# Keeping one and a half V tiles instead of one between two decoder layers, with reordered visits and smaller helper operations

## The chip, the cores and the metric

The kernel runs on one core of one Trainium2 chip. The metric is the device time of one execution, in microseconds (us). Executions of most of the kernels here agree within about 0.1%, so medians of four or more runs are compared. Each round of experiments ran on one chip beside runs of the kernel before; kernels of different rounds ran on different chips, and are compared because the kernel before agreed there (medians 2558.78 to 2559.24 us).

## The reference

Two blocks, A (attention over a cache) and B (a feed-forward network), run alternately, twice, on 8 rows of 640 numbers. Both attention blocks read the same caches: 8 batches x 32 heads x 4096 keys x 128, bf16, for K and for V, 536.9 MB.

```python
def _A_ref(x, k_cache, v_cache, wq, wo):
    q = (x @ wq).reshape(B, Sq, Hq, Dh).transpose(0, 2, 1, 3)     # Sq = 1, 32 heads of 128
    scores = jnp.einsum("bhqd,bhkd->bhqk", q, k) * (Dh ** -0.5)
    o = jnp.einsum("bhqk,bhkd->bhqd", _softmax(scores), v)
    return o.transpose(0, 2, 1, 3).reshape(B, Sq, Hq * Dh) @ wo
def _B_ref(x, w1, w2):
    return jnp.maximum(x @ w1, 0) @ w2                              # 640 -> 1728 -> 640
x = A_x
x = x + _A_ref(_layernorm(x), ...);  x = x + _B_ref(_layernorm(x), ...)
x = x + _A_ref(_layernorm(x), ...);  x = x + _B_ref(_layernorm(x), ...)
```

## The kernel before

The work is a list of 256 visits: 2 layers x 8 batches x 16 pairs of heads. A visit needs a K tile and a V tile of 2 MB each (128 partitions x 64 keys x 128). They pass through a ring of four slots of 16 KB per partition. DVE multiplies the K tile by the query in place; PE sums it ("folds" it) with identity matmuls; a softmax over two visits follows; three visits later PE applies the weights to V ("attend"). A batch's layer-1 visits are put among the next batch's layer-0 visits, and the V tile of pair 15 stays on chip from layer 0 to layer 1, so that layer 1 need not load it.

```python
KEEP = 1
...
def load_v(v):
    layer, b, hp = visits[v]
    if hp in keep:
        if layer == 1:
            V_tiles[v] = kept.pop((b, hp))
            return
        V_tiles[v] = kept[b, hp] = rpool.tile([P, J, Dh], BF16, name=f"V_keep{keep.index(hp)}")
    else:
        V_tiles[v] = kv.tile([P, J, Dh], BF16, name="V_sb", tag="kv")
    nc.sync.dma_start(out=V_tiles[v], in_=pair_src(A_v_cache, b, hp))
...
    for i in range(NV + LAG):            # LAG = 3, v = i - LAG   (cut: conditions)
        mult/fold(i, parts 0, 1)
        reduce_s(i - 1); softmax_a(blk); softmax_d(v // 2); scale_o(v - 1); add_y(v - 2)
        mult/fold(i, parts 2, 3)
        load_first(i, v)                 # K tile i + 2, into the slot of K tile i
        softmax_b(blk)
        o_sb = attend(v)
        load_second(i, v)                # V tile v + 2, into the slot of V tile v
        softmax_c(blk); gather_o(v, o_sb); project_o(v - 1)
```

A K slot comes free when its last fold ends; a V slot when its attend ends.

## Time and profile before

| | before |
|---|---|
| time, median of 13 runs in all | 2558.92 us |
| DMA: bytes, share of 16 engines' span | 1071.93 MB, 99.4% |
| rate from 165 to 2500 us | 425 GB/s |
| DVE wait for K tiles | 1013.8 us, 4.0 us per visit |
| last V tile landed, to the end of the span | 2539.40 us, 17.60 us |

First the page of the kernel before. The digits are busy tenths in 40 equal slices, GB/s is what DMA moved in each; then come the data queue (packets, MB, share of 16 engines' span) and the chain of work that ended last, by engine.

```profile
span 2557.0 us, 36318 instructions
PE 1922.1 (75%) x15406; PEld 867.4 (34%) x15406; DVE 1484.9 (58%) x2451; ACT 512.8 (20%) x1604; POOL 2.0 (0%) x15
...
DMA  9999999999999999999999999999999999999996
GB/s 395 415 413 426 427 426 426 426 426 420 426 427 424 424 423 426 426 422 426 423 426 426 426 420 427 425 426 425 419 427 425 426 425 420 427 427 425 425 419 292
...
q1 hardware_dynamic: 81808, 1071.93, 99.4%
...
DMA 61%; PE 22%; DVE 14%; issue 2%; ACT 1%; SPq 0%; DVEq 0%; ACTq 0%
```

DMA is full in every slice but the last; PE and DVE are not. The chain shows 61% for DMA because it steps through load, multiply, fold and next load of the same slot.

The timeline of the end (start us, us, what, and in brackets the idle time before it) shows the serial tail:

```profile
2539.40 1.91 PE L365 MATMUL o_ps<-V_sb,P 128*8 128x512 bf16 x16 [1.66 <-DMA V_sb<-in_A_v_cache_dram]
...
2542.06 1.28 ACT L162 ACT_TABLE_LOAD   x1
...
2545.76 0.26 ACT L162 ACTIVATE lnv<-ch_ps,eps_c 128x1 f32<-128x1 f32 x1 [2.42 <-PE ch_ps L157]
2546.04 1.28 ACT L164 ACT_TABLE_LOAD   x1
2547.33 0.20 ACT L164 ACTIVATE rstd<-lnv 128x1 f32<-128x1 f32 x1
...
2554.66 0.31 SPq L510 DMA_DIRECT2D out_dram<-xo  x1
```

Of the two activation-table loads the first is done while others work; the second stands in the chain.

### The profile page before, as it was taken

To read this page: it belongs to the slowest core of one execution; us is meant where nothing else is said; L and a number is where in the kernel's file an instruction comes from. 1 tells how busy PE (TensorE), PEld (TensorE's weight loads), DVE (VectorE), ACT (ScalarE), POOL (GpSimd) and SP (SyncE) were. 2 spreads that over 40 slices of the span, in tenths; PEclk is the share of its full clock that TensorE was granted. 3 is DMA by queue.
4 is the path that set the end of the run, shared out by engine and by line. 5 is a ranking of instruction groups with operands and counts; after the bars stand their busy time and mean duration, and the time that the engine had idled before them with its cause. 6 is when DMAs were issued, how large, how long until landed. Compare 5 with 4: busy or idle time off the path is not lost.

```text
span 2557.0 us, 36318 instructions
## 1 busy us (share of the span) xinstructions
PE 1922.1 (75%) x15406; PEld 867.4 (34%) x15406; DVE 1484.9 (58%) x2451; ACT 512.8 (20%) x1604; POOL 2.0 (0%) x15
## 2 busy tenths in 40 slices
PE   6657776787777867778777787778777788777776
PEld 2223332343333423334333343333333244323333
DVE  5446565656656556556566565555565565655653
ACT  1112221122112212122111221112221122112212
POOL 0000000000000000000000000000000000000000
PEclk8878888898989888888888888888888888888887
DMA  9999999999999999999999999999999999999996
GB/s 395 415 413 426 427 426 426 426 426 420 426 427 424 424 423 426 426 422 426 423 426 426 426 420 427 425 426 425 419 427 425 426 425 420 427 427 425 425 419 292
DMA packets 81970, 1074.24 MB, mean 420 GB/s; under 512 B 8256, under 2 KB 14096, under 8 KB 17296
## 3 DMA queue, kind: packets, MB, share of 16 engines
q1 hardware_dynamic: 81808, 1071.93, 99.4%
q8 instruction: 120, 1.97, 0.3%
q14 instruction: 42, 0.34, 0.0%
HBM read 1071.88 MB, written 0.01 MB: 419 GB/s over the span
## 4 chain that ended last, share of the span: by engine, by line
DMA 61%; PE 22%; DVE 14%; issue 2%; ACT 1%; SPq 0%; DVEq 0%; ACTq 0%
DMA K_sb<-in_A_k_cache_dram 60%; PE s_ps L303 18%; DVE K_sb L293 12%; DVE S_sb L314 1%; PE o_ps L365 1%; PE q_ps L277 1%; ACT P L341 1%; PE ch_ps L208 1%; DMA V_sb<-in_A_v_cache_dram 0%; ACT o_sb L370 0%; DVE mrow L318 0%; PE ch_ps L188 0%; PE blk_ps L320 0%; PE blk_ps L332 0%; PE y_ps L389 0%
## 5 line engine op out<-in xcount | busy, mean ns | idle before, releaser
L293 DVE TENSOR_TENSOR K_sb<-K_sb,qb 128x2048 bf16<-128x2048 bf16 x1024 | 1205.7, 1220 | 1018.1 <-DMA K_sb<-in_A_k_cache_dram 1013.8
L303 PE MATMUL s_ps<-K_sb,ident_b 128*128 128x512 bf16 x4096 | 1266.7, 458 | 379.8 <-DVE K_sb L293 359.0
L303 PEld LDWEIGHTS <-ident_b 128*128 128x128 bf16 x4096 | 452.7, 113 | 1064.0 <-issue 695.4
L370 ACT CAST o_sb<-o_ps 104x512 bf16<-104x512 f32 x256 | 149.8, 585 | 807.0 <-PE o_ps L365 802.9
L365 PE MATMUL o_ps<-V_sb,P 128*8 128x512 bf16 x3840 | 258.0, 381 | 2.1 <-DMA V_sb<-in_A_v_cache_dram 2.1
L334 ACT ACTIVATE nmax<-blk_ps 128x4 f32<-128x4 f32 x128 | 22.2, 173 | 1067.2 <-PE blk_ps L332 1067.2
L341 ACT ACTIVATE P<-S_sb,nmax 64x64 bf16<-64x64 f32 x512 | 186.8, 365 | 9.1
L314 DVE TENSOR_REDUCE S_sb<-s_ps 128x64 f32<-128x512 f32 x256 | 175.1, 684 | 3.6 <-PE s_ps L303 2.3
L376 PE MATMUL oT_ps<-dsel,o_sb 104*128 104x2 bf16 x1024 | 64.4, 167 | 115.9 <-ACT o_sb L370 115.9
L348 PE MATMUL blk_ps<-lrow,ones_f 128*128 128x4 f32 x256 | 49.9, 265 | 119.3 <-ACT P L341 119.3
L365 PEld LDWEIGHTS <-P 128*8 128x8 bf16 x4096 | 98.7, 86 | 95.2 <-issue 47.6
L376 PEld LDWEIGHTS <-o_sb 104*128 104x128 bf16 x1024 | 44.2, 98 | 183.8 <-ACT o_sb L370 183.6
L389 PE MATMUL y_ps<-oT,wo_sb 128*128 128x1 bf16 x2560 | 99.8, 163 | 0.3 <-DVE oT L381 0.3
L348 PEld LDWEIGHTS blk_ps<-lrow,ones_f 128*128 128x128 f32 x256 | 38.7, 191 | 176.0 <-ACT P L341 173.5
L341 ACT ACTIVATION_READ_ACCUMULATOR P<-S_sb,nmax 64x1 f32 x512 | 94.6, 185 | 0.0
L389 PEld LDWEIGHTS <-wo_sb 128*128 128x128 bf16 x2560 | 82.5, 96 | 0.4 <-DVE oT L381 0.4
L282 ACT CAST qb<-q_ps 128x512 bf16<-128x512 f32 x64 | 37.4, 585 | 141.0 <-PE q_ps L277 141.0
L332 PEld LDWEIGHTS blk_ps<-diag,ones_f 2*128 2x128 f32 x256 | 37.4, 182 | 54.6 <-issue 48.7
L277 PE MATMUL q_ps<-wq_sb,xln 128*64 128x512 bf16 x320 | 53.0, 474 | 2.7 <-DMA wq_sb<-in_A_wq_dram 2.7
L332 PE MATMUL blk_ps<-diag,ones_f 2*128 2x4 f32 x256 | 48.7, 258 | 0.6 <-DVE diag L328 0.6
L277 PE MATMUL q_ps<-wq_sb,xq 128*64 128x512 bf16 x320 | 46.1, 423 | 0.0
L320 PE MATMUL blk_ps<-ident_f,mrow 128*2 128x128 f32 x128 | 45.9, 358 | 0.0
(53 smaller groups left out, 561.7 us busy)
## 6 DMA issues: line engine op xcount, KB each, us to landing
K_sb<-in_A_k_cache_dram SPq DMA_DIRECT2D x256, 2048.0 KB, 12.9
V_sb<-in_A_v_cache_dram SPq DMA_DIRECT2D x240, 2048.0 KB, 16.5
V_keep<-in_A_v_cache_dram SPq DMA_DIRECT2D x8, 2048.0 KB, 17.2
wq_sb<-in_A_wq_dram SPq DMA_DIRECT2D x4, 1280.0 KB, 19.0
wo_sb<-in_A_wo_dram SPq DMA_DIRECT2D x4, 1280.0 KB, 24.7
w_sb<-in_B_w_dram SPq DMA_DIRECT2D x1, 2160.0 KB, 28.0
w_sb<-in_B_w_dram SPq DMA_DIRECT2D x1, 2080.0 KB
w_sb<-in_B_w_dram SPq DMA_DIRECT2D x1, 80.0 KB, 31.1
```

The lines of the kernel that those rows point to most:

```text
L277: nc.tensor.matmul(q_ps[hh * HP : (hh + 1) * HP], lhsT=_free(xl[:, c, col : col + 1], [(0, HP)]), rhs=wv[:, c, g, :, hh, :], start=(c == 0 ...
L293: nc.vector.tensor_tensor(out=kk, in0=kk, in1=_free(qb_tiles[i][:, lo : lo + DW], [(0, J), (1, DW)]), op=ALU.mult)
L303: nc.tensor.matmul(s_tiles[i], lhsT=ident_b, rhs=K_tiles[i][:, :, lo : lo + RW], start=(part == 0 and k == 0), stop=(part == NQT - 1 and k ...
L314: nc.vector.tensor_reduce(out=S_tiles[k][:, j, :], in_=s_tiles.pop(i), axis=AX.X, op=ALU.add)
L320: nc.tensor.transpose(out=blk_ps[k][:2, :P], in_=mrow, identity=ident_f)
L332: nc.tensor.matmul(gmax, lhsT=ones_f[:2, :], rhs=diag.rearrange("n j h -> n (j h)"), start=True, stop=True)
L341: nc.scalar.activation(out=P2[k % 2][r, j, :, hh], in_=S[r, j, :], func=ACT.Exp, bias=nmax[r, j, hh : hh + 1], scale=inv_sqrt_dh, accum_ou ...
L348: nc.tensor.matmul(L_ps, lhsT=ones_f, rhs=lrow2[k % 2].rearrange("p j h -> p (j h)"), start=True, stop=True)
L365: nc.tensor.matmul(o_ps[32 * c : 32 * c + 8, :], lhsT=P2[k % 2][:, j, 4 * g : 4 * g + 4, :], rhs=V[:, 4 * g : 4 * g + 4, :], start=(g < 4) ...
L370: nc.scalar.copy(out=o_sb, in_=o_ps[:104, :])
L376: nc.tensor.matmul(oTp_tiles[v], lhsT=o_sb[:, i, :], rhs=dsel[:104, i, :], start=(i == 0), stop=(i == 3))
L389: nc.tensor.matmul(y_tiles[v][:, c : c + 1], lhsT=wo_sb[:, 2 * hp + hh, c * P : (c + 1) * P], rhs=oT[:, hh : hh + 1], start=(hh == 0), sto ...
```

## The change

The intent: fewer bytes. Besides pair 15's V tile, half of pair 14's stays on chip (32 of 64 keys per partition, 8 KB). To make room, small buffers shrink (identity and ones in bf16 or as one column, fewer double buffers). At the same time the visit is reordered: all multiplies and folds of a visit run back to back, the last 32 columns as two parts of 16, and the small operations follow. Layer norm takes a square root and a reciprocal instead of logarithm and exponential; the softmax maximum goes through PE in bf16; the transposes of input and output become one matmul each.

```diff
-KEEP = 1
+KEEP = ((0, 64), (1, 32))
+PARTS = (32, 32, 32, 16, 16)
@@ load_v
-        if hp in keep:
-            if layer == 1:
-                V_tiles[v] = kept.pop((b, hp))
-                return
-            V_tiles[v] = kept[b, hp] = rpool.tile(...)
-        else:
-            V_tiles[v] = kv.tile(...)
-        nc.sync.dma_start(out=V_tiles[v], in_=pair_src(A_v_cache, b, hp))
+        kk = keep.get(hp, 0)
+        src = pair_src(A_v_cache, b, hp)
+        pieces = []
+        if kk and layer == 0:
+            kept[b, hp] = rpool.tile([P, kk, Dh], BF16, name=f"V_keep{hp}")
+            nc.sync.dma_start(out=kept[b, hp], in_=src[:, :kk, :])
+        if kk:
+            pieces.append((0, kk, kept[b, hp]))
+        if kk < J:
+            V = kv.tile([P, J, Dh], BF16, name="V_sb", tag="kv")
+            nc.sync.dma_start(out=V[:, kk:, :], in_=src[:, kk:, :])
+            pieces.append((0, J, V))
+        V_tiles[v] = pieces
@@ layer norm
-            nc.scalar.activation(out=lnv, in_=st["var"], func=ACT.Ln, bias=eps_c, scale=1.0 / D)
-            nc.scalar.activation(out=r, in_=lnv, func=ACT.Exp, scale=-0.5)
+            nc.scalar.activation(out=st["std"], in_=st["var"], func=ACT.Sqrt, bias=eps_c, scale=1.0 / D)
+            nc.vector.reciprocal(out=rstd, in_=st["std"])
@@ the visit, in order (cut: conditions)
-  mult/fold(parts 0, 1); reduce_s; softmax_a; softmax_d; scale_o; add_y(v - 2); mult/fold(parts 2, 3)
-  load_first; softmax_b; attend; load_second; softmax_c; gather_o; project_o
+  score(i)  (five parts, back to back); take_q; load_first; softmax_c; attend; load_second
+  reduce_s; softmax_a; softmax_d; scale_o; project_o; softmax_b; add_y(v - 1); project_q; gather_o
... (cut: bf16 identity and ones, x as [P, B, DC], one PSUM tile for o and y, single transposes)
```

More of the change, by code (lines that the diff above doesn't have):

```diff
@@ L72 @@
     w2_sb = wres.tile([P, FC, D], BF16, name="w2_sb")
-    x_bf = sm.tile([B, D], BF16, name="x_bf", tag="row", bufs=1)
-    nc.sync.dma_start(out=x_bf, in_=A_x.rearrange("b s d -> (b s) d"))
+    x_bf = sm.tile([B * DC, P], BF16, name="x_bf", tag="row", bufs=1)
+    nc.sync.dma_start(out=x_bf, in_=A_x.rearrange("b s (c p) -> (b s c) p", p=P))
     wq_sb = wres.tile([P, DC, HD], BF16, name="wq_sb")
@@ L97, in load_w2 @@
             nc.sync.dma_start(out=w2_sb[: Dff % P, n_full, :], in_=B_w2[n_full * P : Dff, :])
-    ident_f = consts.tile([P, P], FP32, name="ident_f")
-    nc.gpsimd.memset(ident_f, 0.0)
+    ident = consts.tile([P, P], BF16, name="ident")
+    nc.gpsimd.memset(ident, 0.0)
     nc.gpsimd.affine_select(
-        out=ident_f, in_=ident_f, pattern=[[-1, P]], compare_op=ALU.not_equal,
+        out=ident, in_=ident, pattern=[[-1, P]], compare_op=ALU.not_equal,
         fill=1.0, base=0, channel_multiplier=1,
     )
-    ident_b = consts.tile([P, P], BF16, name="ident_b")
-    nc.vector.tensor_copy(out=ident_b, in_=ident_f)
-    ones_f = consts.tile([P, P], FP32, name="ones_f")
-    nc.vector.memset(ones_f, 1.0)
+    ones_c = consts.tile([P, 1], FP32, name="ones_c")
+    nc.vector.memset(ones_c, 1.0)
+    ones_f = _free(ones_c, [(0, P)])
+    onesb_c = consts.tile([P, 1], BF16, name="onesb_c")
+    nc.vector.memset(onesb_c, 1.0)
+    ones_b = _free(onesb_c[:2], [(0, P)])
     eps_c = consts.tile([P, 1], FP32, name="eps_c")
@@ L123, with mean, center @@
     nc.vector.memset(o_ps, 0.0)
-    xT = consts.tile([P, DC, B], FP32, name="xT")
-    outT = consts.tile([P, DC, B], BF16, name="outT")
+    xT = consts.tile([P, B, DC], FP32, name="xT")
+    outT = consts.tile([P, B, DC], BF16, name="outT")
     def ln_steps(b0, nb, xln):
         st = {}
+        x = xT[:, b0 : b0 + nb, :]
         def sums():
-            s1 = sm.tile([P, nb], FP32, name="s1")
-            nc.vector.tensor_reduce(
-                out=s1, in_=xT[:, :, b0 : b0 + nb].rearrange("p c b -> p b c"), axis=AX.X, op=ALU.add
-            )
-            st["s1"] = s1
-        def mean():
-            mean_ps = ps.tile([P, nb], FP32, name="ch_ps")
-            nc.tensor.matmul(mean_ps, lhsT=ones_f, rhs=st["s1"], start=True, stop=True)
-            st["mean"] = mean_ps
-        def center():
-            xc = sm.tile([P, DC, nb], FP32, name="xc")
-            nc.vector.scalar_tensor_tensor(
-                out=xc, in0=_free(st["mean"], [(0, DC), (1, nb)]), scalar=-1.0 / D, in1=xT[:, :, b0 : b0 + nb],
-                op0=ALU.mult, op1=ALU.add,
-            )
-            sq = sm.tile([P, DC, nb], FP32, name="sq")
+            st["s1"] = sm.tile([P, nb], FP32, name="s1", bufs=1)
+            nc.vector.tensor_reduce(out=st["s1"], in_=x, axis=AX.X, op=ALU.add)
+        def mean():
+            st["mean"] = ps.tile([P, nb], FP32, name="ch_ps")
+            nc.tensor.matmul(st["mean"], lhsT=ones_f, rhs=st["s1"], start=True, stop=True)
+        def center():
+            xc = sm.tile([P, nb, DC], FP32, name="xc", bufs=1)
+            nc.vector.scalar_tensor_tensor(
+                out=xc, in0=_free(st["mean"], [(1, nb), (0, DC)]), scalar=-1.0 / D, in1=x, op0=ALU.mult, op1=ALU.add
+            )
+            sq = sm.tile([P, nb, DC], FP32, name="sq", bufs=1)
@@ L150, in center @@
             nc.vector.tensor_tensor(out=sq, in0=xc, in1=xc, op=ALU.mult)
-            s2 = sm.tile([P, nb], FP32, name="s2")
-            nc.vector.tensor_reduce(out=s2, in_=sq.rearrange("p c b -> p b c"), axis=AX.X, op=ALU.add)
+            s2 = sm.tile([P, nb], FP32, name="s2", bufs=1)
+            nc.vector.tensor_reduce(out=s2, in_=sq, axis=AX.X, op=ALU.add)
             st["xc"], st["s2"] = xc, s2
         def var():
-            var_ps = ps.tile([P, nb], FP32, name="ch_ps")
-            nc.tensor.matmul(var_ps, lhsT=ones_f, rhs=st["s2"], start=True, stop=True)
@@ L158, in var @@
-            st["var"] = var_ps
-        def rstd():
-            lnv = sm.tile([P, nb], FP32, name="lnv")
-            nc.scalar.activation(out=lnv, in_=st["var"], func=ACT.Ln, bias=eps_c, scale=1.0 / D)
-            r = sm.tile([P, nb], FP32, name="rstd")
-            nc.scalar.activation(out=r, in_=lnv, func=ACT.Exp, scale=-0.5)
-            st["rstd"] = r
+            st["var"] = ps.tile([P, nb], FP32, name="ch_ps")
+            nc.tensor.matmul(st["var"], lhsT=ones_f, rhs=st["s2"], start=True, stop=True)
@@ L167, in scale, with std @@
+        def std():
+            st["std"] = sm.tile([P, nb], FP32, name="std", bufs=1)
+            nc.scalar.activation(out=st["std"], in_=st["var"], func=ACT.Sqrt, bias=eps_c, scale=1.0 / D)
         def scale():
-            nc.vector.tensor_tensor(
-                out=xln, in0=st["xc"], in1=_free(st["rstd"], [(0, DC), (1, nb)]), op=ALU.mult
-            )
-        return [("D", sums), ("P", mean), ("D", center), ("P", var), ("A", rstd), ("D", scale)]
+            rstd = sm.tile([P, nb], FP32, name="rstd", bufs=1)
+            nc.vector.reciprocal(out=rstd, in_=st["std"])
+            nc.vector.tensor_tensor(out=xln, in0=st["xc"], in1=_free(rstd, [(1, nb), (0, DC)]), op=ALU.mult)
@@ L174 @@
+        return [("D", sums), ("P", mean), ("D", center), ("P", var), ("A", std), ("D", scale)]
     xlns = {}
@@ L177, in ffn_steps @@
         st = {}
-        xf = sm.tile([P, DC, 1], BF16, name="xf", bufs=2)
+        xf = sm.tile([P, 1, DC], BF16, name="xf", bufs=1)
         steps = ln_steps(b, 1, xf)
@@ L188, in up @@
                     nc.tensor.matmul(
-                        st["h_ps"][:fs, f : f + 1], lhsT=w1_sb[:, c, f * P : f * P + fs], rhs=xf[:, c, :],
+                        st["h_ps"][:fs, f : f + 1], lhsT=w1_sb[:, c, f * P : f * P + fs], rhs=xf[:, 0, c : c + 1],
                         start=(c == 0), stop=(c == DC - 1),
@@ L193, in relu @@
         def relu():
-            hT = sm.tile([P, FC], BF16, name="hT")
+            hT = sm.tile([P, FC], BF16, name="hT", bufs=1)
             if n_full:
@@ L214, in add @@
             dst = xT if layer == 0 else outT
-            nc.vector.tensor_tensor(out=dst[:, :, b], in0=xT[:, :, b], in1=st["y_ps"], op=ALU.add)
+            nc.vector.tensor_tensor(out=dst[:, b, :], in0=xT[:, b, :], in1=st["y_ps"], op=ALU.add)
         steps += [("P", lambda k=k: up(k)) for k in range(3)] + [("A", relu)]
@@ L219, in ffn_steps @@
         if layer == 0:
-            xq = sm.tile([P, DC, 1], BF16, name="xq", bufs=2)
+            xq = sm.tile([P, 1, DC], BF16, name="xq", bufs=2)
             steps += ln_steps(b, 1, xq)
-            xlns[1, b] = (xq, 0)
+            xlns[1, b] = xq[:, 0, :]
         return steps
@@ L239 @@
     assert NV == 2 * B * NP and NV % 2 == 0
-    keep = order0[NP - KEEP :]
+    keep = {NP - 1 - n: keys for n, keys in KEEP}
     last_of = {}
@@ L243 @@
         last_of[layer, b] = v
-    K_tiles, V_tiles, kept, qb_tiles, s_tiles, S_tiles, invL_tiles, oT_tiles, oTp_tiles, y_tiles = (
+    K_tiles, V_tiles, kept, qb_tiles, s_tiles, S_tiles, invL_tiles, oT_tiles, oy_tiles, q_tiles = (
         {} for _ in range(10)
@@ L259, in load_v @@
         layer, b, hp = visits[v]
-        if hp in keep:
-            if layer == 1:
-                V_tiles[v] = kept.pop((b, hp))
-                return
-            V_tiles[v] = kept[b, hp] = rpool.tile([P, J, Dh], BF16, name=f"V_keep{keep.index(hp)}")
-        else:
-            V_tiles[v] = kv.tile([P, J, Dh], BF16, name="V_sb", tag="kv")
-        nc.sync.dma_start(out=V_tiles[v], in_=pair_src(A_v_cache, b, hp))
+        kk = keep.get(hp, 0)
[11 more added lines that the diff above has]
+        V_tiles[v] = pieces
     def project_q(i):
@@ L271, in project_q @@
         g = hp // GP
-        xl, col = xlns[layer, b]
+        xl = xlns[layer, b]
         q_ps = ps.tile([P, GP, Dh], FP32, name="q_ps")
@@ L277, in project_q, with take_q @@
                 nc.tensor.matmul(
-                    q_ps[hh * HP : (hh + 1) * HP], lhsT=_free(xl[:, c, col : col + 1], [(0, HP)]),
+                    q_ps[hh * HP : (hh + 1) * HP], lhsT=_free(xl[:, c : c + 1], [(0, HP)]),
                     rhs=wv[:, c, g, :, hh, :], start=(c == 0), stop=(c == DC - 1),
                 )
-        qb = sm.tile([P, GP, Dh], BF16, name="qb")
-        nc.scalar.copy(out=qb, in_=q_ps)
+        q_tiles[i] = q_ps
+    def take_q(i):
+        layer, b, hp = visits[i]
+        g = hp // GP
+        qb = sm.tile([P, GP, Dh], BF16, name="qb", bufs=1)
+        nc.scalar.copy(out=qb, in_=q_tiles.pop(i))
         for k in range(i, i + GP):
@@ L285, in project_q, with score @@
             qb_tiles[k] = qb[:, visits[k][2] % GP, :]
-    NQT = 4
-    DW = Dh // NQT
-    def mult(i, part):
-        lo = part * DW
-        kk = K_tiles[i][:, :, lo : lo + DW]
-        nc.vector.tensor_tensor(
-            out=kk, in0=kk, in1=_free(qb_tiles[i][:, lo : lo + DW], [(0, J), (1, DW)]), op=ALU.mult
-        )
-    def fold(i, part):
-        if part == 0:
-            s_tiles[i] = ps.tile([P, J, RW], FP32, name="s_ps", bufs=2)
-        n = DW // RW
-        for k in range(n):
-            lo = part * DW + k * RW
-            nc.tensor.matmul(
-                s_tiles[i], lhsT=ident_b, rhs=K_tiles[i][:, :, lo : lo + RW],
-                start=(part == 0 and k == 0), stop=(part == NQT - 1 and k == n - 1),
-            )
-        if part == NQT - 1:
-            del K_tiles[i], qb_tiles[i]
+    def score(i):
+        s_tiles[i] = ps.tile([P, J, RW], FP32, name="s_ps", bufs=2)
+        K, q = K_tiles.pop(i), qb_tiles.pop(i)
+        lo = 0
+        for w in PARTS:
+            part = K[:, :, lo : lo + w]
+            nc.vector.tensor_tensor(out=part, in0=part, in1=_free(q[:, lo : lo + w], [(0, J), (1, w)]), op=ALU.mult)
+            for k in range(lo, lo + w, RW):
+                nc.tensor.matmul(
+                    s_tiles[i], lhsT=ident, rhs=K[:, :, k : k + RW], start=(k == 0), stop=(k + RW == Dh)
+                )
+            lo += w
+        assert lo == Dh
     def reduce_s(i):
@@ L316, in softmax_a @@
     def softmax_a(k):
-        mrow = sm.tile([P, 2], FP32, name="mrow")
+        mrow = sm.tile([P, 2], BF16, name="mrow")
         nc.vector.tensor_reduce(out=mrow, in_=S_tiles[k], axis=AX.X, op=ALU.max)
         blk_ps[k] = ps.tile([P, P + 8], FP32, name="blk_ps")
-        nc.tensor.transpose(out=blk_ps[k][:2, :P], in_=mrow, identity=ident_f)
+        nc.tensor.matmul(blk_ps[k][:2, :P], lhsT=mrow, rhs=ident, start=True, stop=True)
     def softmax_b(k):
@@ L326, in softmax_b @@
         )
-        diag = sm.tile([2, 2, 2], FP32, name="diag")
+        diag = sm.tile([2, 2, 2], BF16, name="diag")
         nc.vector.tensor_tensor(
-            out=diag, in0=_free(ident_f[:2, :2], [(1, 2), (0, 2)]), in1=_free(hmx, [(0, 2), (1, 2)]), op=ALU.mult
+            out=diag, in0=_free(ident[:2, :2], [(1, 2), (0, 2)]), in1=_free(hmx, [(0, 2), (1, 2)]), op=ALU.mult
         )
         gmax = blk_ps[k][:, P : P + 4]
-        nc.tensor.matmul(gmax, lhsT=ones_f[:2, :], rhs=diag.rearrange("n j h -> n (j h)"), start=True, stop=True)
+        nc.tensor.matmul(gmax, lhsT=ones_b, rhs=diag.rearrange("n j h -> n (j h)"), start=True, stop=True)
         nmax = sm.tile([P, 2, 2], FP32, name="nmax")
@@ L359, in attend @@
         k, j = divmod(v, 2)
-        V = V_tiles.pop(v)
+        pieces = V_tiles.pop(v)
         n = J // 4
@@ L363, in attend @@
             c, g = divmod(t, n // 4)
-            g = 4 * g + c
+            lo = 4 * (4 * g + c)
+            V = next(V for k0, nk, V in pieces if k0 <= lo < k0 + nk)
             nc.tensor.matmul(
-                o_ps[32 * c : 32 * c + 8, :], lhsT=P2[k % 2][:, j, 4 * g : 4 * g + 4, :],
-                rhs=V[:, 4 * g : 4 * g + 4, :], start=(g < 4), stop=(g >= n - 4), tile_position=(0, 32 * c),
+                o_ps[32 * c : 32 * c + 8, :], lhsT=P2[k % 2][:, j, lo : lo + 4, :], rhs=V[:, lo : lo + 4, :],
+                start=(g == 0), stop=(g == n // 4 - 1), tile_position=(0, 32 * c),
             )
-        o_sb = sm.tile([104, 4, Dh], BF16, name="o_sb", tag="row", bufs=1)
+        o_sb = sm.tile([104, 4, Dh], BF16, name="o_sb", bufs=1)
         nc.scalar.copy(out=o_sb, in_=o_ps[:104, :])
@@ L373, in gather_o @@
     def gather_o(v, o_sb):
-        oTp_tiles[v] = ps.tile([P, 2], FP32, name="oT_ps")
+        oy_tiles[v] = ps.tile([P, 2 + DC], FP32, name="oy_ps")
         for i in range(4):
-            nc.tensor.matmul(oTp_tiles[v], lhsT=o_sb[:, i, :], rhs=dsel[:104, i, :], start=(i == 0), stop=(i == 3))
+            nc.tensor.matmul(
+                oy_tiles[v][:, :2], lhsT=o_sb[:, i, :], rhs=dsel[:104, i, :], start=(i == 0), stop=(i == 3)
+            )
     def scale_o(v):
@@ L380, in scale_o @@
         oT_tiles[v] = sm.tile([P, 2], BF16, name="oT")
-        nc.vector.tensor_tensor(out=oT_tiles[v], in0=oTp_tiles.pop(v), in1=invL_tiles[k][:, j, :], op=ALU.mult)
+        nc.vector.tensor_tensor(out=oT_tiles[v], in0=oy_tiles[v][:, :2], in1=invL_tiles[k][:, j, :], op=ALU.mult)
     def project_o(v):
@@ L385, in project_o @@
         oT = oT_tiles.pop(v)
-        y_tiles[v] = ps.tile([P, DC], FP32, name="y_ps")
         for c in range(DC):
@@ L389, in project_o @@
                 nc.tensor.matmul(
-                    y_tiles[v][:, c : c + 1], lhsT=wo_sb[:, 2 * hp + hh, c * P : (c + 1) * P],
+                    oy_tiles[v][:, 2 + c : 3 + c], lhsT=wo_sb[:, 2 * hp + hh, c * P : (c + 1) * P],
                     rhs=oT[:, hh : hh + 1], start=(hh == 0), stop=(hh == 1),
@@ L395, in add_y @@
         layer, b, hp = visits[v]
-        nc.vector.tensor_tensor(out=xT[:, :, b], in0=xT[:, :, b], in1=y_tiles.pop(v), op=ALU.add)
+        nc.vector.tensor_tensor(out=xT[:, b, :], in0=xT[:, b, :], in1=oy_tiles.pop(v)[:, 2:], op=ALU.add)
     NG = NP // GP
@@ L427, in warm @@
     def warm():
-        if WARM:
-            w_ps = ps.tile([P, 512], FP32, name="w_ps", tag="q_ps")
-            for _ in range(WARM):
-                nc.tensor.matmul(w_ps, lhsT=ident_b, rhs=wo_sb[:, 0, :512], start=True, stop=True)
+        w_ps = ps.tile([P, 512], FP32, name="w_ps")
+        for _ in range(WARM):
+            nc.tensor.matmul(w_ps, lhsT=ident, rhs=wo_sb[:, 0, :512], start=True, stop=True)
     LAG = 3
-    o_parts = {}
     with tc.manual_schedule(engines={ENG.PE, ENG.DVE, ENG.Activation, ENG.SP}):
@@ L438 @@
         load_k(1)
-        xT_ps = ps.tile([P, DC, B], BF16, name="ch_ps")
-        for c in range(DC):
-            nc.tensor.transpose(out=xT_ps[:, c, :], in_=x_bf[:, c * P : (c + 1) * P], identity=ident_b[:B, :B])
-        nc.vector.tensor_copy(out=xT, in_=xT_ps)
-        xln0 = consts.tile([P, DC, B], BF16, name="xln0")
+        xT_ps = ps.tile([P, B * DC], FP32, name="ch_ps")
+        nc.tensor.matmul(xT_ps, lhsT=x_bf, rhs=ident[: B * DC, : B * DC], start=True, stop=True)
+        nc.vector.tensor_copy(out=xT, in_=xT_ps.rearrange("p (b c) -> p b c", b=B))
+        xln0 = consts.tile([P, B, DC], BF16, name="xln0")
         for _, step in ln_steps(0, B, xln0):
@@ L446 @@
         for b in range(B):
-            xlns[0, b] = (xln0, b)
+            xlns[0, b] = xln0[:, b, :]
         project_q(0)
+        take_q(0)
         for i in range(NV + LAG):
@@ L454 @@
             if new:
-                for part in range(NQT // 2):
-                    mult(i, part)
-                    fold(i, part)
+                score(i)
+                for f in late.get(i, []):
+                    f()
+            if i + 1 in q_tiles:
+                take_q(i + 1)
+            load_first(i, v)
+            if v >= 0 and v % 2 == 0:
+                softmax_c(v // 2)
+            if v >= 0:
+                o_sb = attend(v)
+            load_second(i, v)
             if 1 <= i <= NV:
@@ L465 @@
                 scale_o(v - 1)
-            if v - 2 >= 0:
-                add_y(v - 2)
-                if last_of[visits[v - 2][:2]] == v - 2:
-                    chain += ffn_steps(*visits[v - 2][:2])
+                project_o(v - 1)
             slot()
-            if new:
-                for part in range(NQT // 2, NQT):
-                    mult(i, part)
-                    fold(i, part)
-                for f in late.get(i, []):
-                    f()
-            load_first(i, v)
             if blk is not None:
                 softmax_b(blk)
+            if v - 1 >= 0:
+                add_y(v - 1)
+                if last_of[visits[v - 1][:2]] == v - 1:
+                    chain += ffn_steps(*visits[v - 1][:2])
             slot()
-            if v >= 0:
-                o_sb = attend(v)
-            load_second(i, v)
-            slot(early=False)
-            if blk is not None:
-                softmax_c(blk)
-            if v >= 0:
-                gather_o(v, o_sb)
-            if v - 1 >= 0:
-                project_o(v - 1)
             slot(early=False)
@@ L493 @@
                 project_q(i + 2)
-            if new and v >= 0:
-                warm()
-        add_y(NV - 2)
+            if v >= 0:
+                gather_o(v, o_sb)
+                if new:
+                    warm()
         scale_o(NV - 1)
@@ L503 @@
             step()
-        for c in range(DC):
-            if c == 0:
-                r_ps = ps.tile([B, DC, P], BF16, name="q_ps")
-            nc.tensor.transpose(out=r_ps[:, c, :], in_=outT[:, c, :], identity=ident_b)
-        xo = sm.tile([B, DC, P], BF16, name="xo", tag="row", bufs=1)
+        r_ps = ps.tile([B * DC, P], FP32, name="ch_ps")
+        nc.tensor.matmul(r_ps, lhsT=outT.rearrange("p b c -> p (b c)"), rhs=ident, start=True, stop=True)
+        xo = sm.tile([B * DC, P], BF16, name="xo", tag="row", bufs=1)
         nc.vector.tensor_copy(out=xo, in_=r_ps)
-        nc.sync.dma_start(out=out.rearrange("b s (c p) -> (b s) c p", p=P), in_=xo)
+        nc.sync.dma_start(out=out.rearrange("b s (c p) -> (b s c) p", p=P), in_=xo)
 _INS = ['A_x', 'A_k_cache', 'A_v_cache', 'A_wq', 'A_wo', 'B_x', 'B_w1', 'B_w2']
```

## The prediction

> **What bounds the kernel now.** The core's DMA engines. The overview by slices shows them nine tenths busy or more in every slice but the last; the queue table gives the data queue 99.4% of 16 engines' span, for 1071.93 MB. From 165 to 2530 us the windows view reads 425 GB/s, DMA share 1.01, with PE busy for 77% and DVE for 59%. The Trainium skill ("DMA: Bandwidth & Descriptors", Specifications) puts the fabric ceiling at 435 GB/s; this trace's plateau of 426 to 428 agrees to 2%. The chain of waits gives DMA only 61%, because it walks through a K tile's reuse (load 12.9 us, multiply, fold, next load); but a load takes that long because it queues behind others, so I trust the saturation. After the last V tile lands at 2539.4 us comes a serial tail of 17.6 us.
>
> **What the change does.**
> 1. Bytes. Besides the V tile of head pair 15, half the V tile of pair 14 stays on chip from layer 0 to layer 1: 8 batches x 1,048,576 B = 8.39 MB less, leaving about 1063.5 MB. At 425 GB/s that is 19.7 us, all on the bound. The half tiles come as 8 KB instead of 16 KB packets; estimated from the first 165 us, where 15 MB of weights in packets of 1 to 3 KB cost about 3 us extra, 1024 more packets cost under 0.5 us.
> 2. K release. The multiplies of a visit run without the reduce and small ops between them (0.6 to 1.1 us in the timeline) and end in two parts of 16 columns, so a K slot comes free about 1 us sooner. DMA has a queue anyway: I allow 0 to 5 us from dips (a few 10 us windows at 390 to 410 GB/s).
> 3. PE and ScalarE. One bf16 pass for two fp32 passes in the max transpose and broadcast; one output matmul for five; square root and reciprocal for Ln and Exp. Mid-kernel this is hidden. In the tail the second table load goes (1.28 us in the trace; the Trainium skill, "ScalarE: Activation LUTs", What ACT_TABLE_LOAD costs, says about 1283 ns, which agrees), a 0.17 us reciprocal comes, projection and add of the visit before the last leave the chain (about 0.4), and output transposes (0.70) and copy (0.48) shrink by about 0.6. Sum: about 2.2 us.
> 4. Fewer buffers (one qb, joined o/y bank): new waits of at most a cast, 0.58 us, while DVE waits for K anyway (3.7 to 4.5 us per visit late in the timeline).
>
> **Predicted time.** 2558.7 - 19.7 - 2.2 + 0.5 = 2537.3, say 2537 us (0.85% faster). Eight in ten: 2530 to 2543. Faster by over 2%: 0.01; within 2%: 0.97; slower by over 2%: 0.02.
>
> **What would show it.**
> - Queue table: 1063.5 MB, share 99% or more; 423 to 427 GB/s in the middle.
> - From the last V tile's landing to the end: about 15.4 us, with one table load, off the chain.
> - DVE's wait for K loads stays its largest and rises; K issue-to-landing rises above 12.9 us, since it is issued earlier into the same queue. Busy times of PE and DVE change by a few per cent without moving the time.
>
> **What would make it wrong.** Engines idle between transfers where I read queueing: then the earlier K release pays more, 2515 us or below. Or bunched folds and waits leave PE more often at half clock (fold matmul 0.43 against 0.22 us), K slots free later than the queue drains, and the DMA share falls under 98%. Or the pair with half its V resident needs less DMA than compute, and the two buffers don't cover it.

## More of the kernel before

The program fixes by hand the order in which each engine's work is listed.

From the waits of the kernel before (engine, line, waited for: us in total, times, longest), and from its DMA issues (count, KB each, median us from issue to landing):

```profile
DVE K_sb L293 <- DMA K_sb<-in_A_k_cache_dram: 1013.8, 246, 12.8
...
DVE oT L381 <- PE oT_ps L376: 5.4, 6, 3.2
DVE xT L396 <- PE y_ps L389: 5.2, 2, 4.7
DVE invL L354 <- PE blk_ps L348: 2.9, 1, 2.9
...
K_sb<-in_A_k_cache_dram SPq DMA_DIRECT2D x256, 2048.0 KB, 12.9
```

DVE waits for K tiles and for almost nothing else.

## The result and the profile after

The changed kernel takes 2537.96 us (median of 8 runs, 2537.69 to 2538.80) against 2558.92 us. Ratios are the mean time of one kernel's runs over that of the other's of the same rounds, so not quite the ratio of the medians quoted; here it is 0.9917 (95% interval 0.9908 to 0.9927): 0.8% faster.

The page of the changed kernel, the same lines as above:

```profile
span 2536.9 us, 36375 instructions
PE 1867.7 (74%) x15270; PEld 872.9 (34%) x15270; DVE 1538.2 (61%) x2732; ACT 504.6 (20%) x1578; POOL 2.0 (0%) x15
...
DMA  9999999999999999999999999999999999999997
GB/s 395 414 413 426 426 424 427 426 425 425 416 426 425 427 426 420 426 425 426 427 412 427 426 426 426 420 425 426 425 425 424 426 426 424 415 427 427 416 427 310
...
q1 hardware_dynamic: 83028, 1063.54, 99.4%
...
DMA 66%; PE 23%; DVE 11%; issue 0%; ACT 0%; SPq 0%; DVEq 0%; ACTq 0%
```

The bytes fell by 8.39 MB and nothing else of this moved. Its waits and K loads:

```profile
DVE K_sb L298 <- DMA K_sb<-in_A_k_cache_dram: 446.0, 235, 10.5
DVE hmx L320 <- PE blk_ps L316: 239.5, 128, 3.3
DVE xT L394 <- PE oy_ps L387: 140.8, 129, 4.1
DVE invL L350 <- PE blk_ps L344: 133.7, 128, 2.9
...
K_sb<-in_A_k_cache_dram SPq DMA_DIRECT2D x256, 2048.0 KB, 13.2
```

This is the surprise. DVE's wait for K tiles fell from 1013.8 to 446.0 us, where the prediction said it would rise. In its place DVE now waits 514 us (239.5 + 140.8 + 133.7) for results of PE; before, the same waits cost it 5.2 us for xT and 2.9 for invL, and none for hmx is listed. The sum of both, 960 us, is not far from the 1027 us of the four lines shown for before. The likely reason, read from the program's order and not tested by itself: the reorder brought DVE's small operations close behind the PE work that feeds them; before, multiplies stood between the two, so that PE had delivered by then. So a visit now leaves DVE 446.0 / 256 = 1.7 us of free time instead of 4.0 us. This cost no time here (keep_one below), but it is a reserve spent.

The end of the changed kernel, in its timeline:

```profile
2521.65 1.91 PE L362 MATMUL o_ps<-V_sb,P 128*8 128x512 bf16 x16 [1.99 <-DMA V_sb<-in_A_v_cache_dram]
...
2524.31 1.28 ACT L160 ACT_TABLE_LOAD   x1
...
2527.64 0.26 ACT L160 ACTIVATE std<-ch_ps,eps_c 128x1 f32<-128x1 f32 x1 [2.05 <-PE ch_ps L156]
...
2534.64 0.32 SPq L497 DMA_DIRECT2D out_dram<-xo  x1
```

The last V tile lands 17.75 us earlier (2539.40 to 2521.65), and the tail from there to the end of the span shrinks from 17.60 to 15.25 us, 2.35 us. One table load is left in it, and ScalarE does it while it would be idle.

### The profile page after: what moved, and what is told of

Same layout as the page of the kernel before. It is cut to its first block, busy times and chain, and to the rows that moved or that the text cites. A ratio compares the mean times of both kernels' runs of the same rounds, so it can differ in the third digit from the quotient of the medians.

```text
span 2536.9 us, 36375 instructions
## 1 busy us (share of the span) xinstructions
PE 1867.7 (74%) x15270; PEld 872.9 (34%) x15270; DVE 1538.2 (61%) x2732; ACT 504.6 (20%) x1578; POOL 2.0 (0%) x15
## 3 DMA queue, kind: packets, MB, share of 16 engines
q1 hardware_dynamic: 83028, 1063.54, 99.4%
## 4 chain that ended last, share of the span: by engine, by line
DMA 66%; PE 23%; DVE 11%; issue 0%; ACT 0%; SPq 0%; DVEq 0%; ACTq 0%
DMA K_sb<-in_A_k_cache_dram 65%; PE s_ps L300 21%; DVE K_sb L298 11%; PE o_ps L362 1%; DMA V_sb<-in_A_v_cache_dram 1%; PE ch_ps L203 0%; PE oy_ps L387 0%; PE blk_ps L344 0%; PE q_ps L277 0%; ACT o_sb L367 0%; PE ch_ps L183 0%; DVE xT L394 0%; DVE hmx L320 0%; PE blk_ps L316 0%; PE oy_ps L373 0%
## 5 line engine op out<-in xcount | busy, mean ns | idle before, releaser
L300 PE MATMUL s_ps<-K_sb,ident 128*128 128x512 bf16 x4096 | 1267.4, 469 | 566.8 <-DVE K_sb L298 545.0
L298 DVE TENSOR_TENSOR K_sb<-K_sb,qb 128x2048 bf16<-128x2048 bf16 (+1 forms) x1280 | 1203.0, 1006 | 446.0 <-DMA K_sb<-in_A_k_cache_dram 446.0
L300 PEld LDWEIGHTS <-ident 128*128 128x128 bf16 x4096 | 470.3, 115 | 1264.6 <-issue 766.0
L320 DVE TENSOR_REDUCE hmx<-blk_ps 2x2 f32<-2x128 f32 x128 | 35.7, 279 | 239.5 <-PE blk_ps L316 239.5
L394 DVE TENSOR_TENSOR xT<-xT,oy_ps 128x5 f32<-128x5 f32 x256 | 38.6, 151 | 140.8 <-PE oy_ps L387 140.8
L350 DVE RECIPROCAL invL<-blk_ps 128x4 f32<-128x4 f32 x128 | 23.4, 183 | 133.7 <-PE blk_ps L344 133.7
L387 PE MATMUL oy_ps<-oT,wo_sb 128*128 128x1 bf16 x2560 | 103.1, 165 | 0.3 <-DVE oT L380 0.3
L373 PE MATMUL oy_ps<-dsel,o_sb 104*128 104x2 bf16 x1024 | 64.3, 166 | 36.6 <-ACT o_sb L367 36.6
L344 PEld LDWEIGHTS blk_ps<-lrow,ones_c 128*128 128x128 f32 x256 | 48.8, 191 | 20.2 <-ACT P L337 1.9
L203 PE MATMUL ch_ps<-hT,w_sb 128*128 128x1 bf16 x1120 | 43.1, 165 | 2.0 <-ACT hT L194 0.3
L203 PEld LDWEIGHTS <-w_sb 128*128 128x128 bf16 x1120 | 40.1, 96 | 9.4 <-PE oy_ps L387 5.5
## 6 DMA issues: line engine op xcount, KB each, us to landing
K_sb<-in_A_k_cache_dram SPq DMA_DIRECT2D x256, 2048.0 KB, 13.2
```

The lines of the kernel that those rows point to most:

```text
L203: nc.tensor.matmul(st["y_ps"][:, c : c + 1], lhsT=w2_sb[:fs, f, c * P : (c + 1) * P], rhs=st["hT"][:fs, f : f + 1], start=(f == 0), stop=( ...
L298: nc.vector.tensor_tensor(out=part, in0=part, in1=_free(q[:, lo : lo + w], [(0, J), (1, w)]), op=ALU.mult)
L300: nc.tensor.matmul(s_tiles[i], lhsT=ident, rhs=K[:, :, k : k + RW], start=(k == 0), stop=(k + RW == Dh))
L344: nc.tensor.matmul(L_ps, lhsT=ones_f, rhs=lrow2[k % 2].rearrange("p j h -> p (j h)"), start=True, stop=True)
L373: nc.tensor.matmul(oy_tiles[v][:, :2], lhsT=o_sb[:, i, :], rhs=dsel[:104, i, :], start=(i == 0), stop=(i == 3))
L387: nc.tensor.matmul(oy_tiles[v][:, 2 + c : 3 + c], lhsT=wo_sb[:, 2 * hp + hh, c * P : (c + 1) * P], rhs=oT[:, hh : hh + 1], start=(hh == 0) ...
```

## The experiments

Twelve kernels ran, all with correct results. The kernel before took 2558.8 to 2559.2 us beside them.

### keep_one: the new schedule without the saved bytes

```diff
-KEEP = ((0, 64), (1, 32))
+KEEP = ((0, 64),)
```

> The changed kernel with the half V tile of pair 14 no longer kept: all of the new schedule, none of the saved bytes (1071.93 MB again). Bytes theory (the time is bytes over the DMA rate, plus a tail): 2538.0 + 8.39 MB / 425 GB/s = 2557.2 us, less 0 to 0.5; only the tail's 2.2 us below the kernel before. Schedule theory (the time comes from K slots that free earlier and from cheaper PE and ScalarE work): near 2538 to 2542 us.

Measured: 2556.54 us (2556.46 to 2556.72), against 2559.24 for the kernel before; ratio 0.9989, interval 0.9975 to 1.0004, which alone does not tell the 2.7 us from nothing. The trace does. Its data queue and its last V tile:

```profile
q1 hardware_dynamic: 81876, 1071.93, 99.5%
...
2539.43 1.91 PE L362 MATMUL o_ps<-V_sb,P 128*8 128x512 bf16 x16 [1.98 <-DMA V_sb<-in_A_v_cache_dram]
```

The last V tile lands at 2539.43 us; in the kernel before it was 2539.40. These are one trace each, and executions of the kernel before differ by up to 2.3 us; but the new schedule does nothing for the stream that could be told from this scatter, far from the 17 to 21 us of the schedule theory. The span ends at 2554.7 us, so the tail is the short one of the changed kernel, 15.3 us. The schedule theory has fallen. From here to the changed kernel it is 18.6 us for 8.39 MB.

### bytes_only: the saved bytes without the new schedule

In the kernel before, 20 keys of pair 14 are kept too, by the changed kernel's loading function (32 do not fit beside that kernel's larger small buffers, which shows what shrinking them was for).

```diff
-KEEP = 1
+KEEP = ((0, 64), (1, 20))
... (load_v and attend take V in pieces, as in the change)
```

> The kernel before, with nothing changed but that 20 of 64 keys per row of pair 14's V stay on chip too (32 do not fit beside its larger small buffers). It moves 8 x 655,360 B = 5.24 MB less. Bytes theory: 2558.9 - 12.3 = 2546.6 us, give or take 1. Schedule theory: no change, 2558 to 2559 us.

Measured: 2548.00 us (2547.76 to 2549.45), ratio 0.9957 (0.9942 to 0.9972). 11.2 us for 5.24 MB, where 12.3 were expected (the median lies 0.4 us outside the 1 us that I allowed) and the rival expected none. Bytes alone make the kernel faster, by 91% of what was expected. split_v below prices more than half of the rest.

### split_v: the same bytes in twice as many V loads

```diff
-            nc.sync.dma_start(out=V[:, kk:, :], in_=src[:, kk:, :])
+            for k0 in range(kk, J, 32):
+                nc.sync.dma_start(out=V[:, k0 : k0 + 32, :], in_=src[:, k0 : k0 + 32, :])
```

> The changed kernel with every V load of 16 KB rows issued as two loads of 8 KB rows into the same tile: same bytes, same slots, 28,672 more packets. It tells why v_half3 came to 2585 instead of 2518. If the 8 KB packets cost what that kernel's excess over its bytes would ask (66 us over 29,950 packets and 16 engines, an estimate of 35 ns each): about 2600 us. If packets are nearly free (my estimate in the prediction: under 0.5 us per 1024) and the missing half slot was to blame: 2538 to 2552 us.

Measured: 2557.33 us (2557.09 to 2558.20), 19.4 us above the changed kernel: between the two expectations. Its packets and queue:

```profile
DMA packets 115450, 1065.89 MB, mean 417 GB/s; under 512 B 12052, under 2 KB 17876, under 8 KB 21076
...
q1 hardware_dynamic: 115284, 1063.55, 99.6%
```

The queue holds 32,256 more packets than the changed kernel's 83,028: 224 splits x 128 rows, and 16 packets under 512 B for each of the 224 added loads. So a split of one V tile into two loads costs 19.4 / 224 = 0.087 us, or 9.6 ns per packet and engine. (The figure of 10.8 ns in a later expectation counts the 28,672 row packets alone.) The change adds 8 such splits, 0.7 us: the prediction's "under 0.5" was a little low. With it, 8.39 MB should give 19.7 - 0.7 = 19.0 us (18.6 measured), and 5.24 MB 12.3 - 0.7 = 11.6 us (11.2 measured).

### late_k2 and before_late2: the same delay in both schedules

Two added DVE operations per visit take the maximum of a part of the K tile with itself, in place, ahead of its multiply. The result is unchanged, and each takes 1.2 us. (The first edit is written out here; in the runs a table names the parts.)

```diff
             part = K[:, :, lo : lo + w]
+            if lo in (0, 32):      # late_k2, in the changed kernel; late_k1: only lo == 0
+                nc.vector.tensor_tensor(out=part, in0=part, in1=part, op=ALU.max)
```
```diff
         kk = K_tiles[i][:, :, lo : lo + DW]
+        if part < 2:               # before_late2, in the kernel before
+            nc.vector.tensor_tensor(out=kk, in0=kk, in1=kk, op=ALU.max)
```

> The changed kernel with two extra in-place DVE operations (max of a part with itself, result unchanged) ahead of the first two multiplies of every visit, so that every K slot comes free up to about 2.4 us later if one costs what a multiply costs (1.2 us). DVE then has some 8.4 of 9.85 us per visit to do. Saturation theory: DMA has a load queued all the time, so at most +5 us (2538 to 2543). If the chain of waits is literal (K load, multiply, fold, next load in series, one loop per two visits): 128 x 2.4 = about +300 us.

> The kernel before with the same two extra DVE operations per visit as late_k2 (2.4 us). In the kernel before DVE waits for K loads 1014 us, 4.0 us per visit. Slack theory: 2.4 is less than 4.0, so 2559 to 2575 us, although late_k2 lost 306 us with the same addition: the change used up more than half of the schedule's slack. Literal chain: about 2559 + 300 us, as in late_k2.

Measured: late_k2 2844.36 us (2843.49 to 2845.64), 306 us more than the changed kernel. My expectation of at most 5 us was wrong, and the literal chain's 300 was met. So I asked whether it was met for the chain's reason. before_late2 took 2608.88 us (2607.31 to 2616.72), only 50 us more than the kernel before: neither the literal chain's 300 nor my 0 to 16. In late_k2 (from its page: queue and chain; then waits):

```profile
q1 hardware_dynamic: 83028, 1063.54, 93.3%
...
PE 48%; DVE 47%; DMA 2%; issue 1%; SPq 1%; DVEq 0%; ACT 0%; ACTq 0%
...
DVE hmx L323 <- PE blk_ps L319: 295.0, 128, 3.5
DVE invL L353 <- PE blk_ps L347: 178.0, 128, 2.8
DVE xT L397 <- PE oy_ps L390: 141.6, 129, 4.4
DVE K_sb L300 <- DMA K_sb<-in_A_k_cache_dram: 24.4, 7, 7.2
```

and in before_late2 (its waits):

```profile
DVE K_sb L294 <- DMA K_sb<-in_A_k_cache_dram: 409.4, 230, 10.3
```

In late_k2 DMA has left the chain (2%): the chain now runs through DVE and PE, each in its own order. DVE's wait for K is used up (446.0 to 24.4 us) and its waits for PE grew by 101 us (514 to 614.6). The added operations, 622 us, less the 422 us of wait they filled, plus those 101 us, give 301 of the 306 us. PE was slower there as well: a fold took 509 ns in the mean against 469, at a mean granted clock of 0.791 against 0.848. How much of the 101 us comes from that was not separated. In the kernel before the same operations found 1014 us of waiting and took 604 of it. The chain's number was right in late_k2 by coincidence: what counts is how much delay each schedule absorbs before DMA starves, and the changed one absorbs less.

The two kernels differ in more than the order: late_k2 also keeps the half tile of pair 14. That is not what makes the difference. Take the time from one visit's first multiply (or added operation) to the next visit's, in the four traces, for the 155 visits that lie away from resident V (not among the ten from the visit before pair 15's layer-1 visit on, nor among the first 20). It rose from 9.90 us in the changed kernel to 10.98 in late_k2, and from 9.90 us in the kernel before to 10.09 in before_late2: 1.08 us lost per visit against 0.20. Which part of the change (order, buffers or smaller operations) took the slack was not varied by itself. Of before_late2's 50 us, 31 arise in these visits, 16 in the 80 around resident V and 3 in the first 20. Since 2.4 us is less than the mean wait of 4.0 us, the slack can't be spread evenly; why the 50 us arise was not settled.

### late_k1 and late_k1_none: half the delay, with and without resident V

> The changed kernel with one extra DVE operation (1.2 us) ahead of each visit's multiplies, where late_k2 had two and cost 306 us. In the changed kernel DVE waits for K loads 446 us, 1.7 us per visit. Slack theory (DMA bounds; the in-order compute of a visit takes 9.85 - 1.7 us; only what exceeds the slack costs time): 1.2 is less than 1.7, so 2538 to 2548 us. Literal chain (every delay of a K release adds to a serial loop): half of late_k2's cost, about 2690 us.

Measured: 2570.22 us (2566.01 to 2570.64), 32 us more than the changed kernel. Far from the chain's 150, but more than the slack theory allows. The slices show where (page of late_k1):

```profile
GB/s 394 416 411 427 426 395 427 427 425 426 387 427 426 425 424 393 427 425 426 423 399 427 425 426 426 399 426 425 423 406 412 427 425 423 398 420 427 394 424 309
```

There is a hole about every fifth slice, eight in all: one for each batch's layer-1 visits, which begin with the pairs whose V is resident. Closer, late_k1 by windows (length; busy us of PE, PEld, DVE, ACT, POOL; granted clock; DMA share; GB/s) and DVE's timeline:

```profile
665.00:670.00 5.00, 2.64 (x12) 0.99 (x13) 4.90 (x6) 0.24 (x1) 0.00 (x0) 0.83 0.87 352
670.00:675.00 5.00, 4.69 (x42) 2.04 (x41) 2.88 (x9) 0.76 (x3) 0.00 (x0) 0.83 0.41 107
```
```profile
665.00 1.23 DVE L300 TENSOR_TENSOR K_sb<-K_sb 128x2048 bf16<-128x2048 bf16 x1
...
674.54 1.21 DVE L300 TENSOR_TENSOR K_sb<-K_sb 128x2048 bf16<-128x2048 bf16 x1
```

DVE begins visits at 665.00 and 674.54 us without any idle time before them: K was there, and compute was late. They are the fourth and fifth visits after that of pair 15, whose V is resident. DMA moved 107 GB/s for the 5 us from 670 on. A visit whose V is resident asks DMA for 2.1 MB, 4.9 us at 425 GB/s, while a visit's compute takes 9.5 us here (674.54 - 665.00). So I tried the same delay with nothing resident:

```diff
-KEEP = ((0, 64), (1, 32))
+KEEP = ()
```

> late_k1 (one extra DVE operation of 1.2 us per visit) with no V kept at all, so that every visit loads 4.2 MB: 1088.71 MB. Where did late_k1's 32 us go? If only to the visits with resident V, where DMA has less to do than compute: this kernel costs its bytes alone, 2556.5 (keep_one) + 16.78 MB x 2.35 us = 2596 us, to 2600. If the extra 1.2 us costs time in all visits: 32 us more, about 2628 us.

Measured: 2595.33 us (2595.28 to 2595.37), what its bytes alone should cost (2596 us, an estimate: a run of this kernel without the delay was not made). Its slices have no holes:

```profile
GB/s 394 416 414 425 426 428 423 425 425 424 425 426 422 426 427 425 423 427 423 422 426 426 426 422 427 421 427 426 422 426 426 426 425 422 426 423 426 426 422 312
```

So 1.2 us per visit is absorbed wherever both tiles are loaded, and late_k1's 32 us are eight holes of about 4 us at resident V: by the starts of visits, the 80 visits there take 33 us more than in the changed kernel, and the 155 away from them 3 us less. This also bears out, for the delayed kernel, the prediction's last warning, of the pair with resident V needing less DMA than compute.

### apart, even48, even24: does the changed kernel already pay for that?

The changed kernel's slices show faint dips (412 to 420) at six of these eight places. Three kernels with the same saved bytes give the compute time to catch up, or spread the resident keys.

```diff
-    order1 = [NP - 1, NP - 3, NP - 2, NP - 4] + order0[:-GP]
+    order1 = [NP - 1, NP - 3, NP - 4, NP - 2] + order0[:-GP]          # apart, even48
-KEEP = ((0, 64), (1, 32))
+KEEP = ((0, 48), (1, 48))                                             # even48
+KEEP = ((0, 24), (1, 24), (2, 24), (3, 24))                           # even24 (old order1)
```

> The changed kernel with the layer-1 order of the first four pairs 15, 13, 12, 14 instead of 15, 13, 14, 12: the two visits that need less DMA than compute (whole and half of V resident) lie three visits apart instead of two. The changed kernel's GB/s dips below 400 once per layer-1 block (about 4 us in all more than keep_one, where only pair 15 is resident). If the visits with resident V starve DMA because the compute of about 8 us cannot catch up in between: 2535 to 2537 us. If the dips are something else: 2538 us.

> As apart, and the same bytes kept, but 48 of 64 keys of both pairs 15 and 14 instead of 64 and 32, so that no visit needs less than 2.5 MB (6.2 us of DMA against about 8 us of compute). Resident-visit theory: another 1 to 2 us less, minus 0.7 us for 1024 more packets: 2533 to 2537 us. Otherwise 2538 to 2539 us.

> The changed kernel with the same bytes kept as 24 of 64 keys of each of pairs 12 to 15: each of the four visits then needs 3.3 MB, 7.9 us of DMA, about what compute takes, so DMA should have no dip at all. Resident-visit theory: about 4 us gained, 2 us lost to 3,072 more packets (10.8 ns each over 16 engines, from split_v): 2535 to 2537 us, and the 10 us windows under 400 GB/s gone from the layer-1 blocks. Otherwise 2540 us (packets alone).

Measured: apart 2538.01 us (2537.68 to 2538.63), even48 2540.70 (2540.12 to 2541.50), even24 2546.36 (2543.91 to 2547.15). The resident-visit theory misses in all three; apart meets its other figure, 2538 us, and even48 and even24 miss both of theirs. Nothing is gained by moving the visits apart, and spreading the keys costs 2.7 and 8.4 us. But the three kernels did not remove the dips: away from start and end, their lowest slices are 414, 414 and 407 GB/s, where the changed kernel has 412. So what removing them would give was not tested. It could not be much for the half tile: this already pays 18.6 of the 19.0 us that bytes and packets give. Compared with the changed kernel, even48 has 16 more loads (2,304 packets) and even24 32 (4,608): 1.4 and 2.8 us at split_v's price. (The 3,072 packets in even24's expectation left out 1,536.) The rest is open. A guess, untested: a wholly resident tile takes no ring slot, which leaves K loads a slot more, and a partly resident one does not.

### v_half3 and ring3: still more V kept, at the expense of the ring

v_half3 loads V as half tiles through three slots of 8 KB, beside two K slots of 16 KB, and keeps the whole V tile of pair 14. ring3 has three slots of 16 KB for both, and keeps pairs 15 and 14 whole and half of 13; with three slots the program also loads V first and only one visit ahead (its own code for that case).

```diff
-KEEP = ((0, 64), (1, 32))                               # v_half3
+KEEP = ((0, 64), (1, 64))
+VKEYS = 32
+VBUFS = 3
-    kv = ctx.enter_context(tc.tile_pool(name="kv", bufs=RING))
+    kv = ctx.enter_context(tc.tile_pool(name="kv", bufs=2))
+    vp = ctx.enter_context(tc.tile_pool(name="vp", bufs=VBUFS))
-        if kk < J:   ... (cut: the load of V in one piece)
+        for k0 in range(kk, J, VKEYS):
+            V = vp.tile([P, VKEYS, Dh], BF16, name="V_sb", tag="v")
+            nc.sync.dma_start(out=V, in_=src[:, k0 : k0 + VKEYS, :])
... (cut: attend finds its keys in these pieces)
-RING = 4                                                # ring3
-KEEP = ((0, 64), (1, 32))
+RING = 3
+KEEP = ((0, 64), (1, 64), (2, 32))
```

> The changed kernel with the V tiles streamed as halves through three 8 KB slots instead of two 16 KB slots, and the 8 KB won used to keep the whole V tile of pair 14: 8.39 MB less again (1055.15 MB). If the DMA queue still never runs dry with one half tile less of prefetch: 2538.0 - 19.7 = 2518 us, give or take 4. If that prefetch space was what kept DMA fed, the share of the data queue falls below 99% and the time is at or above 2538 us.

> The changed kernel with three 16 KB slots for K and V instead of four, and the 16 KB won used to keep the V tiles of pairs 15 and 14 whole and half of 13's: 12.58 MB less (1050.96 MB). If three slots kept DMA fed: 2538.0 - 29.6 = 2508 us. Slack theory: a visit's compute of about 8 us now sits between two loads with only one tile loading meanwhile, so DMA runs dry in each visit; its share falls well below 95% and the time rises above 2600 us.

Measured: v_half3 2584.80 us (2576.93 to 2595.05), ring3 2675.96 us (2672.59 to 2677.14). Both move fewer bytes and are slower than both kernels. Their queues, v_half3 first, then ring3:

```profile
q1 hardware_dynamic: 112980, 1055.16, 98.8%
```
```profile
q1 hardware_dynamic: 81876, 1046.76, 96.3%
```

(My expectation for ring3 had a slip: 64 more keys are kept, so 16.78 MB and 39 us, not 12.58 MB and 29.6 us.) v_half3's 29,952 more packets are 208 splits, 18 us at split_v's price. The other 49 us of its distance from 2518 have two possible causes, the missing half slot and the second visit with its whole V resident, and they were not varied one at a time. By the starts of visits of one trace each, v_half3's 80 visits around resident V take 11 us more than those of split_v, although the 8.39 MB that they save are worth 19.7 us; the other visits, the start and the end add 18 us. So most of the 49 us arise where V is resident, and the missing prefetch is felt there first. ring3 has no more packets than keep_one, and DMA's share falls to 96.3%, not to the "well below 95%" that I had expected; the time above 2600 us was met. Its loss lies not only at resident V: the 155 visits away from it, which load both tiles in both kernels, take 10.53 us against 9.91 in keep_one. In these two kernels prefetch space was worth more than kept data. None of the twelve beats the changed kernel.

## Why the prediction was right, and where it was not

- **Bytes on the bound (right).** 1063.54 MB came out as predicted. 19.7 us less 0.5 for packets was forecast, and 18.6 us was measured from keep_one to the changed kernel. bytes_only shows it without the new schedule, at 11.2 us for 5.24 MB.
- **DMA saturated (right; its reach too wide).** Share 99.4% before and after, 425 and 424 GB/s from 165 to 2500 us. But "DMA has a queue anyway" holds only within a small reserve: late_k1, late_k2, v_half3 and ring3 all leave it.
- **Earlier K release buys almost nothing (right).** keep_one's last V tile landed within 0.03 us of the kernel before's. The allowance of 0 to 5 us from dips was not needed. The issue-to-landing time of a K load rose from 12.9 to 13.2 us, so in the direction predicted, but by 0.3 us where I had counted on a release about 1 us sooner. The traces bear out the 0.3: from a visit's first multiply to the end of its last fold the median is 6.83 us before and 6.52 after. The size of this term was wrong, and it did not matter.
- **The tail (right).** 2.2 us predicted, 2.35 us in the traces; 15.4 us predicted, 15.25 measured, with one table load off the chain. 18.6 + 2.35 is 20.95 us; the medians differ by 20.96. That they agree so closely is luck, since executions of one kernel differ by up to 2.3 us.
- **Wrong: "DVE's wait for K loads stays its largest and rises".** It stayed the largest single wait, but fell to 446.0 us. I counted the gaps that the reorder takes out between multiplies, and did not follow what the small operations would wait for behind the folds. These waits take 1.0 to 1.9 us each (239.5 / 128, 133.7 / 128, 140.8 / 129) and 514 us in all. ("New waits of at most a cast" was said of the fewer buffers alone, which no run varied.) They cost nothing in this kernel; but with the same added delay the changed kernel loses 306 us where the kernel before loses 50.
- **"Busy times change by a few per cent" (right).** PE 1922.1 to 1867.7 us, DVE 1484.9 to 1538.2 us.

The total was 2537 us predicted, 2537.96 us measured.

## What to carry to other kernels

In a stream that keeps DMA busy for 99% of the time, predict from bytes over the rate that the trace shows, and add the serial tail by itself. A reorder of compute may then show nothing in the time, as here, yet spend the reserve that keeps DMA fed: compare how long the engine that consumes the stream (here DVE) waits for loads, before and after, and test the reserve with a deliberate delay. Keeping data on chip paid here while the four prefetch slots were left alone, and did not where they were cut down; and in late_k1 the reserve was used up first around the visits whose V was already on chip.

## What the Trainium skill lacked or had wrong

- "DMA: Bandwidth & Descriptors", Where 436 GB/s comes from, says that for transfers between HBM and on-chip memory the HBM side, about 358 GB/s, is the limit. These runs, of one core, held 425 GB/s from 165 to 2500 us, as in the page's own 16 MB row. The note under its measurements has the condition that the sentence leaves out: they are for one core with its neighbour idle, and about 358 is each core's part when both stream, which no run here tried.
- The same page, Why small descriptors are slow (HBM only), treats descriptors of 256 B. It gives no price for splitting large loads in a saturated stream, and I found none elsewhere. Here splitting a 2 MB load from 16 KB rows into two loads of 8 KB rows cost 0.087 us per split in a saturated stream (19.4 us for 224), and every added load brought 16 packets under 512 B.
- "ScalarE: Activation LUTs", What ACT_TABLE_LOAD costs, adds a drain of about 1380 ns to the load of about 1283 ns. In the tail of the kernel before, the load began 0.02 us after the operation ahead of it ended (2545.76 + 0.26, then 2546.04), took 1.28 us, and the next operation began at 2547.33: a switch cost 1.3 us, with no separate drain to be seen. All 49 loads of that trace that have an operation of ScalarE ahead of them look so: each took 1.28 us, and began 0.02 us after that operation.
- No page that I read says how to measure the reserve of a stream that saturates DMA. The pair late_k2 and before_late2 gives a method and two numbers: 306 and 50 us for the same delay (1.08 and 0.20 us per visit away from resident V).
